# Contiguous destinations for the transposed loads of B and C, and the first x rows in one transfer

## The chip, the cores and the metric

The kernel runs on one core of a Trainium2 chip. The metric is the device time of one execution in microseconds, as a median over runs. Before the change it is 252.53 us, the median of three runs (252.28 to 253.31).

## The reference

A sequence of 2048 tokens with 1024 channels goes through two branches that are mixed by a gate per token, `g = sigmoid(sum(x * gate_w))`; the result is `g * a + (1 - g) * b`.

Branch a is a diagonal state-space layer with complex state of 1024: `Bu = x @ B_bar`, then `h = Lam_bar * h + Bu[t]` over the 2048 tokens, then `y = 2 * Re(h @ C^T) + x * Dskip`. `Lam_bar = exp(dt * Lambda)` and the factor in `B_bar` come from three vectors of length 1024 (`log_dt`, `Lambda_re`, `Lambda_im`).

Branch b picks the 8 tokens with the largest `x @ w_r`, puts only these through a gated expert (`(silu(x w_gate) * (x w_up)) w_down`, hidden size 3584), scales them and adds them to their rows of x.

## The kernel before

The sequence is cut into 8 chunks of 256 tokens, the 1024 channels and the 1024 states into 8 tiles of 128 each. Stage 1 (`s1`, its matmuls are line 253, tile `vps`) multiplies the transposed B, planes re and im, with the transposed x of a chunk; one call `s1(k, cp)` does two state tiles of both planes, 32 matmuls, and ScalarE evicts the PSUM tile to V (line 258). VectorE rotates V by tables (lines 277 to 279), runs the recurrence as a real scan (line 288) and rotates back to H (lines 311 to 315). Stage 2 (`s2`, line 716, tile `zps`) multiplies H with the transposed C, 512 output columns at a time; `s2_last` (line 730) does the last 128 tokens in pieces of 512, 256 and 256 columns. The expert's matmuls (lines 635 and 647), the token selection (lines 501 to 554, tile `fl` among them, read on VectorE at line 533 by `ci`) and the gate columns (`zc`, line 468) are placed between these stages.

The order of the work on TensorE, VectorE, ScalarE and SyncE is written out by hand; each engine runs its list in that order. The main loop over chunks places the pieces by position in a list of pending functions; the first chunks (prologue) are spelled out line by line.

The start matters for the change. SyncE issues, one after the other: the first 256 rows of x as they are (`x0r`, line 77, two transfers), the first two state tiles of B re and B im as transposing transfers (line 89), x of chunks 1 and 2 as transposing transfers (`xT1`, `xT2`, line 85), then the rest of B in pieces of 256 rows and C in pieces of 512 rows (line 98). ScalarE's queue loads the three small vectors into `vrow`. Chunk 0 of x is transposed on TensorE: eight transposes per 128 rows (line 144, tile `xq`), copied to `xT[0]` by ScalarE for the first 128 rows and by VectorE for the second (line 145). Between the two groups stand three small transposes of `vrow` (line 149) and their copy to `vec` on VectorE (line 150). From `vec` follow `dt_b` on ScalarE (line 164), `ang` on VectorE (line 167) and the angle tables (lines 191 to 211). Warm-up matmuls (line 137, tile `wps`) stand ahead of the x transposes (12) and ahead of the first `s1` (7). The prologue's first stage-1 calls are chunk 0, chunk 1 and chunk 2 for the first two state tiles; PSUM has two buffers for `vps`.

BT and CT are one SBUF tile per plane. BT's free dimensions are (channel tile, state); a load of two state tiles writes 256 columns in each of the eight channel tiles, with a step of 1024 elements. CT's are (state tile, output column); a load writes 512 columns in each of eight. The xT tiles are written whole by one transfer each.

The tail of branch b adds the expert rows to the output by one indirect accumulating transfer on GpSimd's queue and reads the last 256 rows back (`ul`, line 703, 128 partitions of two rows).

Of the kernel before, what the change touches and what calls it, by code (L numbers as in the profile page):

```python
# [11 lines left out]
BF16 = mybir.dt.bfloat16  # L12
# [4 lines left out]
P = 128  # L17
LC = 256
# [6 lines left out]
def kernel(  # L25
# [19 lines left out]
    nc = tc.nc  # L45
    _, L, D = A_x.shape
    NP_ = A_B_re.shape[0]
    Fdim = B_w_gate.shape[1]
    NCT = NP_ // P
    KD = D // P  # L50
    NK = L // LC
    NTT = L // P
    BPC = LC // P
    NDH = D // 512
# [4 lines left out]
    x2d = A_x[0]  # L59
    out2d = out[0]  # L60
    Bsrc = (A_B_re, A_B_im)
    Csrc = (A_C_re, A_C_im)

    ctx.enter_context(tc.manual_schedule(engines={mybir.EngineType.PE, mybir.EngineType.DVE, mybir.EngineType.Activation, mybir.EngineType.SP}))
    const = ctx.enter_context(tc.tile_pool(name="const", bufs=1))
# [3 lines left out]
    ps_m = ctx.enter_context(tc.tile_pool(name="ps_m", bufs=2, space=PSUM))  # L69

    xT = [const.tile([P, KD, LC], BF16, name=f"xT{k}", tag=f"xT{k}") for k in range(5)]
    BT = [const.tile([P, KD, NP_], BF16, name=f"BT{pl}") for pl in range(2)]
    CT = [const.tile([P, NCT, D], BF16, name=f"CT{pl}") for pl in range(2)]

    x0r = const.tile([P, BPC, D], BF16, name="x0r", tag="xT5")
    for tl in range(BPC):
        nc.sync.dma_start(x0r[:, tl, :], x2d[tl * P:(tl + 1) * P, :])
    vrow = small.tile([NCT, 5, P], BF16, name="vrow", tag="va")
    for i, v in enumerate((A_log_dt, A_Lambda_re, A_Lambda_im)):
        nc.scalar.dma_start(vrow[:, i, :], v.rearrange("(c p) -> c p", p=P))  # L80
# [5 lines left out]

    def load_B(c0, c1):
        for pl in range(2):
            nc.sync.dma_start_transpose(BT[pl][:, :, c0 * P:c1 * P], Bsrc[pl][c0 * P:c1 * P, :])  # L89

    load_B(0, 2)
    load_xT(1)
# [2 lines left out]
        load_B(c0, c0 + 2)  # L95
    for d0_ in range(0, D, 512):
        for pl in range(2):
            nc.sync.dma_start_transpose(CT[pl][:, :, d0_:d0_ + 512], Csrc[pl][d0_:d0_ + 512, :])

    big_free = [(f"big{i}", "") for i in range(5)]  # L100
    big_tag = {}
# [18 lines left out]
    ident = const.tile([P, P], BF16, name="ident")  # L120
# [20 lines left out]
    for tl in range(BPC):  # L141
        xq = ps_s2.tile([P, KD, P], BF16, name="xq", tag="zps")
        for dc in range(KD):
            nc.tensor.transpose(xq[:, dc, :], x0r[:, tl, dc * P:(dc + 1) * P], ident[:])
        (nc.scalar.copy if tl == 0 else nc.vector.tensor_copy)(out=xT[0][:, :, tl * P:(tl + 1) * P], in_=xq[:])
        if tl == 0:
            va_ps = ps_m.tile([P, 3, NCT], BF16, name="va_ps", tag="m")
            for i in range(3):
                nc.tensor.transpose(va_ps[:, i, :], vrow[:, i, :], ident[:NCT, :NCT])
            nc.vector.tensor_copy(vec[:, 0:3, :], va_ps[:])  # L150
    ldt, lre, lim = vec[:, 0, :], vec[:, 1, :], vec[:, 2, :]


# [93 lines left out]
    def s1u(k, cp, c, pl):  # L247
        if (k, cp) not in vp:
            vp[k, cp] = ps_s1.tile([P, 2, 2, LC], F32, name="vps", tag="vps")
        vps = vp[k, cp]  # L250
        ct = 2 * cp + c
        for dc in range(KD):
            nc.tensor.matmul(vps[:, pl, c, :], lhsT=BT[pl][:, dc, ct * P:(ct + 1) * P], rhs=xT[k][:, dc, :], start=(dc == 0), stop=(dc == KD - 1))  # L253

    def s1e(k, cp):
        if k not in V:
# [451 lines left out]
    def s2(b, dh):  # L708
        k, tl = divmod(b, BPC)
        if dh == 0:  # L710
            ots[b] = opool.tile([P, D], BF16, name="ot", tag="ot")
        dsl = slice(dh * 512, (dh + 1) * 512)
        zps = ps_s2.tile([P, 512], F32, name="zps", tag="zps")
        for ct in range(NCT):
            for pl in range(2):
                nc.tensor.matmul(zps[:], lhsT=H[k][:, pl, ct, tl * P:(tl + 1) * P], rhs=CT[pl][:, ct, dsl], start=(ct == 0 and pl == 0), stop=(ct == NCT - 1 and pl == 1))  # L716
        if dh == 1 and tl == 1:
            big_done("H", k)
        nc.scalar.activation(out=ots[b][:, dsl], in_=zps[:], func=ACT.Copy, scale=gcol[:, b:b + 1])  # L719

    def s2_last(b):
        k, tl = divmod(b, BPC)
        ots[b] = opool.tile([P, D], BF16, name="ot", tag="ot")
        cols = ((0, 512), (512, 256), (768, 256))
        zp = [(ps_s2, ps_s1, ps_s1)[i].tile([P, w], F32, name="zl", tag=("zps", "vps", "vps")[i]) for i, (_, w) in enumerate(cols)]
        for c0 in (0, NCT // 2):
            for i, (d_, w) in enumerate(cols):
                for ct in range(c0, c0 + NCT // 2):
                    for pl in range(2):
                        nc.tensor.matmul(zp[i][:], lhsT=H[k][:, pl, ct, tl * P:(tl + 1) * P], rhs=CT[pl][:, ct, d_:d_ + w], start=(ct == 0 and pl == 0), stop=(ct == NCT - 1 and pl == 1))  # L730
                if c0 and i == 0:
                    nc.scalar.activation(out=ots[b][:, 0:512], in_=zp[0][:], func=ACT.Copy, scale=gcol[:, b:b + 1])
                    fin_half(b, 0)
                elif c0:
                    nc.vector.scalar_tensor_tensor(out=ots[b][:, d_:d_ + w], in0=zp[i][:], scalar=gcol[:, b:b + 1], in1=xts[b][:, d_:d_ + w], op0=ALU.mult, op1=ALU.add)
                    nc.sync.dma_start(out2d[b * P:(b + 1) * P, d_:d_ + w], ots[b][:, d_:d_ + w])
# [147 lines left out]
```

## Time and profile before

| | |
|---|---|
| median of three runs | 252.53 us (252.28 to 253.31) |
| the profiled execution's own time | 252.53 us |
| its span, first to last instruction | 250.8 us |
| TensorE busy | 244.3 us (97%) |
| VectorE busy | 232.9 us (93%) |
| ScalarE busy | 101.6 us (41%) |
| GpSimd busy | 41.3 us (16%) |
| granted TensorE clock | 0.999 |
| chain that ended last | PE 49%, DVE 41%, SP queue 3%, DMA 3%, issue 2% |

PE is TensorE's matmuls, DVE VectorE, ACT ScalarE, POOL GpSimd, SP SyncE; a q behind a name is that engine's queue of instructions or transfers. The chain of waits is followed back from the last instruction: at each step to what released it, or to the instruction before it on its engine. In the timeline the bracket at the end of a line is the idle time of the engine just before it and what ended it. In the windows the columns are busy time and instruction count of PE, weight loads, DVE, ACT and POOL, then the granted clock, the mean busy share of the 16 DMA engines and GB/s. In a tile view the three figures of an instruction are the least, median and greatest duration in ns.

### The profile page before, as it was taken

How to read it: one execution, taken by the hardware profiler on the slowest of the kernel's cores; microseconds unless marked ns; L12 is line 12 of the kernel's file. 1: busy time of each engine (PE TensorE's matmuls, PEld its weight loads, DVE VectorE, ACT ScalarE, POOL GpSimd, SP SyncE). 2: the span in 40 equal slices, each digit the busy share in tenths (PEclk: the TensorE clock that was granted, in tenths of full speed). 3: DMA queues.
4: the chain of work that ended last, by engine and by line, in shares of the span. 5: the costliest groups of instructions: out<-in, count | busy, mean ns of one | idle time of the engine just before them, and what ended most of it. 6: DMA issues, size and time to landing. Idle time of an engine off the chain costs nothing.

```text
span 250.8 us, 4677 instructions
## 1 busy us (share of the span) xinstructions
PE 244.3 (97%) x1986; PEld 164.2 (65%) x1986; DVE 232.9 (93%) x230; ACT 101.6 (41%) x143; POOL 41.3 (16%) x58
## 2 busy tenths in 40 slices
PE   8799999999999999999999999999999999999994
PEld 5688889884678447874487644876448864454453
DVE  1899999999999599999999999999999999999992
ACT  3679981535212322535121372131732335264411
POOL 4020000000000067201400240013101400141520
PEclk9999999999999999999999999999999999999999
DMA  7999999999900202819795587869999829966072
GB/s 182 228 158 238 179 258 211 251 260 261 312 0 3 73 0 89 167 31 348 156 358 190 203 232 236 277 216 338 262 288 293 183 46 277 302 169 178 3 167 84
DMA packets 63492, 48.31 MB, mean 193 GB/s; under 512 B 49504, under 2 KB 51168, under 8 KB 63472
## 3 DMA queue, kind: packets, MB, share of 16 engines
q1 hardware_dynamic: 59056, 37.23, 56.6%
q0 software_dynamic: 4224, 10.53, 17.5%
q8 instruction: 15, 0.25, 0.4%
q10 hardware_dynamic: 192, 0.27, 0.3%
q14 instruction: 5, 0.04, 0.1%
HBM read 27.55 MB, written 8.40 MB: 143 GB/s over the span
## 4 chain that ended last, share of the span: by engine, by line
PE 49%; DVE 41%; SPq 3%; DMA 3%; issue 2%; ACT 0%; DVEq 0%
PE vps L253 22%; PE zps L716 21%; DVE U L288 14%; DVE U L277 4%; DVE U L279 4%; DVE V L278 4%; DVE U L313 4%; DVE H L315 4%; DVE H L311 4%; DVE xt L691 3%; PE zl L730 3%; DMA xT<-in_A_x_dram 3%; SPq L89 2%; PE y L647 1%; PE zc L468 1%
## 5 line engine op out<-in xcount | busy, mean ns | idle before, releaser
L253 PE MATMUL vps<-xT,BT 128*128 128x256 bf16 x1024 | 114.2, 273 | 1.6 <-DMA BT<-in_A_B_re_dram 0.8
L253 PEld LDWEIGHTS <-BT 128*128 128x128 bf16 x1024 | 99.4, 98 | 15.6 <-issue 1.8
L716 PE MATMUL zps<-CT,H 128*128 128x512 bf16 x480 | 105.8, 379 | 0.0
L716 PEld LDWEIGHTS <-H 128*128 128x128 bf16 x480 | 46.3, 98 | 55.7 <-issue 1.9
L288 DVE TENSOR_TENSOR_SCAN U<-d,U 128x2048 bf16<-128x2048 f32 (+1 forms) x20 | 61.7, 3128 | 0.4
L258 ACT CAST V<-vps 128x1024 bf16<-128x1024 f32 x32 | 32.3, 1009 | 60.9 <-PE vps L253 60.9
L719 ACT ACTIVATE ot<-zps,gcol 128x512 bf16<-128x512 f32 x30 | 20.6, 688 | 67.8 <-PE zps L716 65.0
L693 POOL DMA_DIRECT2D out_dram<-xt x14 | 7.8, 561 | 93.1 <-DVE xt L691 92.6
L687 ACT ACTIVATE e<-Dbc,omgcol,gcol 128x1024 f32<-128x1024 bf16 x16 | 18.9, 1233 | 0.0
L691 DVE TENSOR_TENSOR xt<-xt,e 128x1024 bf16<-128x1024 bf16 x16 | 18.8, 1218 | 0.0
L278 DVE TENSOR_TENSOR V<-V,nTi 128x4096 bf16<-128x4096 bf16 (+1 forms) x10 | 16.5, 1652 | 0.5
L277 DVE TENSOR_TENSOR U<-V,T2tab 128x4096 bf16<-128x4096 bf16 (+1 forms) x10 | 16.5, 1645 | 0.5
L279 DVE TENSOR_TENSOR U<-U,V 128x4096 bf16<-128x4096 bf16 (+1 forms) x10 | 16.5, 1652 | 0.3
L554 POOL DMA_INDIRECT xsel<-in_A_x_dram,idx_c x1 | 6.4, 6387 | 61.3 <-ACT ot L719 61.3
L313 DVE TENSOR_TENSOR U<-U,S2tab 128x4096 bf16<-128x4096 bf16 (+1 forms) x8 | 16.2, 2025 | 0.3
L315 DVE TENSOR_TENSOR H<-H,U 128x4096 bf16<-128x4096 bf16 (+1 forms) x8 | 16.2, 2025 | 0.3
L311 DVE TENSOR_TENSOR H<-U,Ctab 128x4096 bf16<-128x4096 bf16 (+1 forms) x8 | 16.1, 2018 | 0.0
L740 POOL DMA_DIRECT2D out_dram<-ot x14 | 14.3, 1048 | 2.0 <-DMA out_dram<-yc,idx_c 2.0
L682 POOL DMA_DIRECT2D xt<-in_A_x_dram x12 | 8.2, 684 | 13.6 <-DMA out_dram<-xt 13.6
L346 DVE TENSOR_TENSOR_SCAN U<-D,U 128x1024 bf16<-128x1024 f32 x4 | 8.9, 2278 | 0.0
L635 PE MATMUL pgu<-wgu,xsel 128*32 128x448 bf16 x128 | 7.4, 355 | 0.0
L730 PE MATMUL zl<-CT,H 128*128 128x256 bf16 (+1 forms) x48 | 7.1, 308 | 0.0
(145 smaller groups left out, 127.9 us busy)
## 6 DMA issues: line engine op xcount, KB each, us to landing
wgu<-in_B_w_gate_dram SPq DMA_DIRECT2D x16, 448.0 KB, 6.4
wgu<-in_B_w_up_dram SPq DMA_DIRECT2D x16, 448.0 KB, 5.7
wd<-in_B_w_down_dram SPq DMA_DIRECT2D x12, 512.0 KB, 6.7
out_dram<-xt POOLq DMA_DIRECT2D x14, 256.0 KB, 2.8
out_dram<-ot POOLq DMA_DIRECT2D x14, 256.0 KB, 5.9
xt<-in_A_x_dram POOLq DMA_DIRECT2D x12, 256.0 KB, 5.1
xt<-in_A_x_dram SPq DMA_DIRECT2D x4, 256.0 KB, 4.1
wd<-in_B_w_down_dram SPq DMA_DIRECT2D x4, 256.0 KB, 7.8
```

Source lines behind the costliest of these rows:

```text
L253: nc.tensor.matmul(vps[:, pl, c, :], lhsT=BT[pl][:, dc, ct * P:(ct + 1) * P], rhs=xT[k][:, dc, :], start=(dc == 0), stop=(dc == KD - 1))
L258: nc.scalar.copy(out=V[k][:, :, 2 * cp:2 * cp + 2, :], in_=vp.pop((k, cp))[:])
L277: nc.vector.tensor_tensor(out=u, in0=v, in1=T2tab[:, :, c0:c1, :], op=ALU.mult)
L278: nc.vector.tensor_tensor(out=v, in0=v, in1=bc(nTi, c0, c1), op=ALU.mult)
L279: nc.vector.tensor_tensor(out=u, in0=u, in1=V[k][:, ::-1, c0:c1, :], op=ALU.add)
L288: nc.vector.tensor_tensor_scan(out=fl, data0=d0[:, c0:c1, :].rearrange("p c t -> p (c t)"), data1=fl, initial=0.0, op0=ALU.mult, op1=ALU.add)
L311: nc.vector.tensor_tensor(out=h, in0=g, in1=bc(Ctab, c0, c1), op=ALU.mult)
L313: nc.vector.tensor_tensor(out=g, in0=g, in1=S2tab[:, :, c0:c1, :], op=ALU.mult)
L315: nc.vector.tensor_tensor(out=h, in0=h, in1=G[k][:, ::-1, c0:c1, :], op=ALU.add)
L691: nc.vector.tensor_tensor(out=xt[:], in0=xt[:], in1=es.pop(b)[:], op=ALU.mult)
L716: nc.tensor.matmul(zps[:], lhsT=H[k][:, pl, ct, tl * P:(tl + 1) * P], rhs=CT[pl][:, ct, dsl], start=(ct == 0 and pl == 0), stop=(ct == NCT ...
L719: nc.scalar.activation(out=ots[b][:, dsl], in_=zps[:], func=ACT.Copy, scale=gcol[:, b:b + 1])
```

## The change

Four edits, all of them in loads and layouts:

- `x0r` is loaded by one transfer of 128 partitions by two rows in place of two transfers of 128 rows.
- The three small transposes of `vrow` and the copy to `vec` come after both groups of x transposes, in place of between them.
- BT's tile is laid out as (pair of state tiles, channel tile, 256 columns), so that each transposing load of B writes one contiguous stretch of each partition; the matmuls of line 253 index it accordingly.
- CT's tile is laid out as (half of the output columns, state tile, 512 columns), with the same effect for the loads of C and the matmuls of stage 2.

The counts of instructions on TensorE, VectorE, ScalarE and GpSimd stay the same; SyncE issues one transfer less. On VectorE the copy of `vec` changes places with the second copy to `xT[0]`.

```diff
-    BT = [const.tile([P, KD, NP_], BF16, name=f"BT{pl}") for pl in range(2)]
-    CT = [const.tile([P, NCT, D], BF16, name=f"CT{pl}") for pl in range(2)]
+    BT = [const.tile([P, NCT // 2, KD, 2 * P], BF16, name=f"BT{pl}") for pl in range(2)]
+    CT = [const.tile([P, NDH, NCT, 512], BF16, name=f"CT{pl}") for pl in range(2)]
 
     x0r = const.tile([P, BPC, D], BF16, name="x0r", tag="xT5")
-    for tl in range(BPC):
-        nc.sync.dma_start(x0r[:, tl, :], x2d[tl * P:(tl + 1) * P, :])
+    nc.sync.dma_start(x0r[:], x2d[0:LC, :].rearrange("(t p) d -> p t d", p=P))
...
-            nc.sync.dma_start_transpose(BT[pl][:, :, c0 * P:c1 * P], Bsrc[pl][c0 * P:c1 * P, :])
+            nc.sync.dma_start_transpose(BT[pl][:, c0 // 2], Bsrc[pl][c0 * P:c1 * P, :])
...
-            nc.sync.dma_start_transpose(CT[pl][:, :, d0_:d0_ + 512], Csrc[pl][d0_:d0_ + 512, :])
+            nc.sync.dma_start_transpose(CT[pl][:, d0_ // 512], Csrc[pl][d0_:d0_ + 512, :])
...
         (nc.scalar.copy if tl == 0 else nc.vector.tensor_copy)(out=xT[0][:, :, tl * P:(tl + 1) * P], in_=xq[:])
-        if tl == 0:
-            va_ps = ps_m.tile([P, 3, NCT], BF16, name="va_ps", tag="m")
-            for i in range(3):
-                nc.tensor.transpose(va_ps[:, i, :], vrow[:, i, :], ident[:NCT, :NCT])
-            nc.vector.tensor_copy(vec[:, 0:3, :], va_ps[:])
+    va_ps = ps_m.tile([P, 3, NCT], BF16, name="va_ps", tag="m")
+    for i in range(3):
+        nc.tensor.transpose(va_ps[:, i, :], vrow[:, i, :], ident[:NCT, :NCT])
+    nc.vector.tensor_copy(vec[:, 0:3, :], va_ps[:])
...
-            nc.tensor.matmul(vps[:, pl, c, :], lhsT=BT[pl][:, dc, ct * P:(ct + 1) * P], rhs=xT[k][:, dc, :], start=(dc == 0), stop=(dc == KD - 1))
+            nc.tensor.matmul(vps[:, pl, c, :], lhsT=BT[pl][:, cp, dc, c * P:(c + 1) * P], rhs=xT[k][:, dc, :], start=(dc == 0), stop=(dc == KD - 1))
...
-                nc.tensor.matmul(zps[:], lhsT=H[k][:, pl, ct, tl * P:(tl + 1) * P], rhs=CT[pl][:, ct, dsl], start=(ct == 0 and pl == 0), stop=(ct == NCT - 1 and pl == 1))
+                nc.tensor.matmul(zps[:], lhsT=H[k][:, pl, ct, tl * P:(tl + 1) * P], rhs=CT[pl][:, dh, ct, :], start=(ct == 0 and pl == 0), stop=(ct == NCT - 1 and pl == 1))
...
-                        nc.tensor.matmul(zp[i][:], lhsT=H[k][:, pl, ct, tl * P:(tl + 1) * P], rhs=CT[pl][:, ct, d_:d_ + w], start=(ct == 0 and pl == 0), stop=(ct == NCT - 1 and pl == 1))
+                        nc.tensor.matmul(zp[i][:], lhsT=H[k][:, pl, ct, tl * P:(tl + 1) * P], rhs=CT[pl][:, d_ // 512, ct, d_ % 512:d_ % 512 + w], start=(ct == 0 and pl == 0), stop=(ct == NCT - 1 and pl == 1))
```

## The prediction

> **What bounds the kernel now.** I read the page's busy shares, then the chain that ended last in order of time, then the timeline of the first 16 us (the only place where the change moves an instruction), and last the tile views of the transposed loads and the windows by stage.
>
> Busy shares: TensorE is the engine with the least room, VectorE next.
>
> ```profile
> PE 244.3 (97%) x1986; PEld 164.2 (65%) x1986; DVE 232.9 (93%) x230; ACT 101.6 (41%) x143; POOL 41.3 (16%) x58
> ```
>
> The chain, in order of time (start, us, what):
>
> ```profile
> 0.74 0.40 SPq L77
> 1.14 0.06 issue
> 1.20 0.42 SPq L77
> 1.62 0.05 issue
> 1.67 2.65 SPq L89
> 4.32 0.05 issue
> 4.37 2.06 SPq L89
> 6.44 0.04 issue
> 6.48 2.11 SPq L85
> 8.58 0.04 issue
> 8.63 6.91 DMA xT<-in_A_x_dram
> 15.54 0.05 issue
> 15.59 24.63 PE vps L253 x224
> ...
> 86.12 0.25 ACT fl L526
> 86.37 0.02 issue
> 86.40 0.28 DVE ci L533
> ```
>
> The reader is to see that the chain enters TensorE at 15.59, when xT2 lands, and that from there TensorE never stops: between 15.6 and 84 us it is busy 68.40 of 68.40 us. At 86.40 the chain passes to VectorE, released by TensorE's work through ScalarE, and returns to TensorE at 194.9. So the time of the whole kernel hangs on when TensorE begins its unbroken run. A later start there is passed on one to one; so is an earlier one.
>
> VectorE has one pause in its stream between 14 and 194 us, and it is the spare room of everything that the change delays:
>
> ```profile
> 86.40 0.28 DVE L533 TENSOR_TENSOR ci<-fl,jrow 8x128 f32<-8x128 f32 x1 [2.45 <-ACT fl L526]
> ```
>
> **The change, part by part.** The sum is made against the profiled execution: span 250.8, its time 252.53, which is also the median of the three runs; 1.73 us lie outside the span.
>
> (a) *One x load in place of two.* SyncE loses one issue, 0.42 + 0.05 = 0.47 us, so every transpose behind it (B, xT1, xT2, then the rest) can be issued up to 0.47 earlier. The chain puts this on the path. But the DMA engines are nearly full then: their share is 0.84 and 0.96 in the windows 2 to 3 and 3 to 4 us (289 and 304 GB/s), and 1.0 to 1.3 in every window from 4 to 13, so the first B transpose stands behind the x rows and each transpose behind the last. The x rows are the same bytes. The gain on xT2's landing is therefore between 0 (the engines are the limit) and 0.47 (the issue is); I take 0.15, near the first, because the full windows are the nearest rows. A loss needs a later landing, below.
>
> When does the merged load land? Before, the halves landed 2.8 us after the issue at 0.74 (3.57) and 3.3 after that at 1.20 (4.5). The ul load has the same shape (128 partitions of 2 rows, 512 KB) and landed after 3.3 us, which gives 4.05; adding 256 KB at 300 GB/s (0.87) to the first landing gives 4.45. I take L = 4.3. The first eight transposes, which started at 3.57, start then; the second eight, which started at 5.02, do not wait for a load of their own any more.
>
> (b) *The transposes of the small vectors behind both x groups.* TensorE before: eight x transposes 3.60 to 4.65, three small ones to 5.08, eight more 5.02 to 5.64, seven warm-up matmuls 5.47 to 6.40. After: sixteen from 4.3 (about 1.05 + 0.62) to 6.0, three small ones (0.5) to 6.5, seven warm-ups (0.93) to 7.4. The first matmuls of L253 started at 7.18, when the first B transpose landed; now they start at about 7.4. Their first half then ends near 9.2, where the second plane's B landed at 9.12, and the group ends near 11.1, before xT1's landing, which was 11.5 and held TensorE up for 0.47. So 0.2 us of delay is eaten by that wait and costs nothing. Without that cover it would cost 0.2.
>
> (c) *VectorE's and ScalarE's start.* VectorE copied vec at 5.12, then the x half at 5.67 to 6.36; ang could start only at 6.28. After, the x half goes first (6.0 to 6.7), vec follows (to about 6.9), dt_b on ScalarE comes 0.29 later and takes 0.21 (to 7.4), ang starts at about 7.45. The tables, and VectorE's whole stream behind them, start about 1.2 us late. Who waits for that? ScalarE: the Sin pair and then the eviction of the first PSUM tile, 12.18 to 13.17, which becomes 13.4 to 14.4; TensorE needs that buffer at 15.3, so 0.9 us remain. ScalarE is caught up at 15.16, where it waited 1.42 for TensorE. VectorE carries the 1.2 on; H of chunk 0 ended at 51.9 and was read at 55.1, H of chunk 1 ended at 75.3 and was read at 81.7 (3.2 and 6.4 to spare), and the 2.45 pause shrinks to about 1.1. Cost: nothing, as long as the delay stays under 2.45.
>
> (d) *Contiguous destinations for B and C.* TensorE reads the same 128-column weights and 512-column operands, contiguous in either layout; its instructions keep their shapes. What is left is the transfer. The kernel has the control in itself: xT tiles are written whole, thus already contiguous, B in pieces of 256 columns with a step of 1024.
>
> ```profile
> L89 SPq DMA_TRANSPOSE BT<-in_A_B_im_dram x4: 1998/2041/2277, 4.4 to 24.1; - x4
> ...
> DMA to landing us min/median/max: 4.7/5.5/6.7
> ```
>
> ```profile
> L85 SPq DMA_TRANSPOSE xT<-in_A_x_dram x7: 1579/2524/2729, 6.5 to 58.8; - x7
> ...
> DMA to landing us min/median/max: 4.6/5.0/5.4
> ```
>
> Same bytes, and the strided ones hold the queue no longer than the contiguous ones (medians 2.04 for one plane of B, 2.55 for the other, 2.52 for xT). Landing is 5.5 against 5.0, partly because two B loads fell into the gap below. I cost this part at nothing; the bounds are 0 and, from the landings, 0.5 per B transpose, two of which stand ahead of xT2: −1.0, which TensorE cannot use in full (below). C is first read at 55 us, long after; nothing there.
>
> The Trainium skill, "DMA: Bandwidth & Descriptors", section "Latency and other measured facts", says that a DMA transpose runs at 261 GB/s with a non-contiguous middle dimension and at about 350 to 400 contiguous. By it the two B transposes would each take some 0.6 us less, and the sum would be the 251.8 of the first rival below; by the rows it is nothing. The same skill's "Trainium Kernel Development and Optimization", section "Best Practices", asks to overlap transfers with compute, which speaks against the merged load: the first eight transposes no longer run under the second half's transfer. By that rule alone the 0.7 us from 3.57 to L would be lost; the waits of (b) cover it.
>
> **Sum.** xT2 lands 0.15 earlier, TensorE's run starts 0.15 earlier, everything behind shifts with it: 252.53 − 0.15 = 252.4. Within 0.5% (1.26 us, about what a measurement of this kernel can tell from no change) on either side by a wide margin.
>
> There is also a floor. TensorE must do two groups of 32 matmuls (3.53 and 3.65 us) and two small transposes (0.2) before xT2's group. With the first group at 7.25 at the earliest (L of 4.05 and the 3.2 us of transposes, vectors and warm-up behind it) the run cannot start before 14.65: at most 0.94 of gain, 0.37%, however fast the transfers get.
>
> **The rivals.**
>
> *Faster transposes.* The contiguous destination, or the earlier issue, really shortens the loads. For it: xT1 and xT2 held TensorE for 0.47 and 0.29, and B for 0.78 and about 0.2. Against it: the two tile views. Price: TensorE from about 7.4 without a wait, 7.4 + 3.53 + 3.65 + 0.2 = 14.8 in place of 15.59, so about −0.75: 251.8. Still within 0.5%. Chance 0.10.
>
> *The merged x load lands late* (the other side). Everything at the start stands behind it: with landing L, TensorE's first group starts at L + 3.1 and must end its two groups by 15.5, so the point is L = 5.0, 0.7 after my value; from there each us costs one, and from L = 5.5 VectorE's 2.45 is gone too. The 512 KB loads of wd took a median of 6.7 us to land under heavy traffic, which bounds it: L = 7.4, 2.4 us later, 254.9. For it: one semaphore now covers twice the bytes, with vector loads of three queues beside it. Against it: the ul row's 3.3 us. It counts as slower (over 1.26) from L = 6.3. Chance 0.07.
>
> *The gap in the transfers falls elsewhere.* In the windows 13 to 14 and 14 to 15 the transfers drop to 68 and 15 GB/s, just as xT2 was finishing; the packet records show a 16 KB packet of the instruction queue (2.0 us) there.
>
> ```profile
> 13.00:14.00 1.00, 1.00 (x11) 0.90 (x10) 0.93 (x10) 0.78 (x3) 0.00 (x0) 1.00 2.27 68
> 14.00:15.00 1.00, 1.00 (x11) 0.79 (x9) 1.00 (x6) 0.00 (x0) 0.00 (x0) 1.00 0.31 15
> ```
>
> If xT2 escapes it, TensorE gains only the 0.29 that it waited: 252.2. If the gap falls ahead of xT1, that lands 2.2 later, at 13.7; 3.65 + 0.2 behind it is 17.6, 2.0 later: 254.5. The packet comes with TensorE's progress, which is still held by xT1's landing, so the order should stay. Chance 0.05 for the bad case.
>
> *Nothing moves at all* (the issue saved is hidden whole): 252.5. It lies inside the forecast.
>
> **How the numbers follow.** Forecast with its variants (252.0 to 252.8): 0.78; faster transposes 0.10 (251.8); late load 0.07 (253.5 to 254.9); displaced gap 0.05 (254.5). Faster by over 0.5% needs more than the floor allows, so only an unseen cause gives it: 0.05, taken out of the first two. Slower by over 0.5%: the two bad cases, some of the late load staying below the bound: 0.10. Same: 0.85. The three runs before spread over 252.28 to 253.31, so the range is 251.6 to 253.4, which leaves out the two bad cases and the unseen gain.
>
> **What would show it.** After: one issue at L77, B's first issue near 1.2; the x transposes starting at 4.0 to 4.5 in one run of sixteen; ang 0.9 to 1.3 later than 6.28; TensorE's unbroken run starting at 15.1 to 15.7; the pause before ci at 0.9 to 1.6 in place of 2.45; B transposes holding the queue 2.0 to 2.6 us as before. It is wrong if B's transposes take 1.5, if the x load lands after 5, or if the pause before ci is gone.

## The result, and the profile after

Measured beside each other, six executions of each, the kernel after takes 253.88 us (253.28 to 254.35) and the kernel before 252.69 (252.28 to 253.31): a ratio of 1.0046, with a 95% interval of 1.0028 to 1.0064. Measured a second time (twelve executions of after, 35 of before) it is 252.84 against 252.59, 1.0025 (1.0006 to 1.0044). The ratios here and below are the recorded ones of the two sets of executions, not quotients of the medians beside them; the medians of the second measurement alone would give 1.0010. By the ratios the change costs 0.25 to 0.46%. That is a small loss, below the 0.5% that the prediction called the same, but both intervals lie above 1, and a gain of 0.15 us was forecast. The first result lies above the range that was given, the second inside it.

The profiled execution of after took 253.81 us with a span of 252.0; before it was 252.53 and 250.8. The span is 1.2 us longer, as the time is (1.28). The counts of instructions have not moved. The busy shares of the page, engine by engine:

```profile
PE 245.4 (97%) x1986; PEld 164.9 (65%) x1986; DVE 233.1 (93%) x230; ACT 101.6 (40%) x143; POOL 41.1 (16%) x58
```

TensorE is busy 1.1 us longer with the same 1986 instructions. That says that something ran slower, not only later. The chain that ended last, of the kernel after, in order of time (start, us, what):

```profile
1.69 5.06 DMA vrow<-in_A_Lambda_im_dram
6.75 0.05 issue
6.80 0.17 PE va_ps L147
6.98 1.40 PE wps L136 x7
8.38 8.12 PE vps L250 x64
16.50 0.13 PE vb_ps L418 x2
16.63 24.56 PE vps L250 x224
```

Before, the chain came through SyncE's queue and the landing of xT2. Now SyncE's transfers are gone from it: from 6.80 on it is TensorE's own work, without a wait. The unbroken run starts about 1 us later (16.63 against 15.59). TensorE's timeline of the same kernel between 3 and 9 us shows the two waits ahead of that (the bracket is the idle time and what ended it):

```profile
4.76 1.07 PE L143 MATMUL xq<-ident,x0r 128*128 128x128 bf16 x16 [0.96 <-DMA x0r<-in_A_x_dram]
5.76 0.20 PE L147 MATMUL va_ps<-ident,vrow 8*128 8x8 bf16 x2
6.80 0.17 PE L147 MATMUL va_ps<-ident,vrow 8*128 8x8 bf16 x1 [0.84 <-DMA vrow<-in_A_Lambda_im_dram]
6.91 1.47 PE L136 MATMUL wps<-wt 128*128 128x256 bf16 x7
8.17 1.06 PE L250 MATMUL vps<-xT,BT 128*128 128x256 bf16 x4
```

The merged x load landed 4.0 us after its issue, and TensorE waited 0.96 for it. Then it waited 0.84 for the third small vector, which before had landed in time. Sixteen x transposes took 1.07, so the clock was full there; the seven warm-up matmuls took 1.47, against 0.93 before. The windows of 1 us of the same kernel tell why (busy time and instruction count of PE, weight loads, DVE, ACT and POOL, then the granted clock, the DMA share and GB/s):

```profile
6.00:7.00 1.00, 0.20 (x2) 0.19 (x3) 0.56 (x1) 0.43 (x1) 0.00 (x0) 1.00 1.04 185
7.00:8.00 1.00, 1.00 (x7) 0.73 (x7) 0.68 (x4) 0.44 (x3) 0.00 (x0) 0.58 1.14 226
8.00:9.00 1.00, 1.00 (x6) 0.72 (x5) 1.00 (x4) 1.00 (x1) 0.44 (x1) 0.50 1.19 253
9.00:10.00 1.00, 1.00 (x7) 0.72 (x5) 0.93 (x3) 0.26 (x1) 0.00 (x0) 0.50 1.23 278
10.00:11.00 1.00, 1.00 (x9) 0.77 (x8) 1.00 (x1) 0.00 (x0) 0.00 (x0) 0.72 1.02 230
11.00:12.00 1.00, 1.00 (x12) 0.90 (x10) 0.93 (x4) 0.95 (x1) 0.00 (x0) 1.00 1.17 267
```

The granted clock of TensorE falls to half from 7.16 to 10.57: by its own records it was full from 3.74, half for 3.41 us, and full from then on. PE is "1.00 busy" in these windows with 6 to 7 matmuls where 12 fit at full clock. A busy share does not show that an engine runs at half rate; the number in brackets and the clock column do.

What the half clock costs can be worked out. At full clock the two groups of 32 matmuls and what stands between them and the run take 7.23 us (7.41 to 14.64 in a kernel below, the base with two loads, whose clock was full there and whose two groups met no wait). Before they took 8.41 (7.18 to 15.59), so 1.18 of it was waiting for B, xT1 and xT2. After they took 8.39 (8.17 to 16.56 in the timeline): no wait is left, and 1.16 of it is the clock. The first group started 0.99 later, the waits gone (−1.18) would have paid for that, and the clock (+1.16) took it back: 0.97. (2.40 us of the two groups lie at half clock, which by itself costs half of that, 1.20.) The last 0.23 of the span's 1.2 is a wait for the expert's `wd` at the end (a group of 56 matmuls took 1.94 at 222.39, and 1.71 before).

VectorE's pause, which the forecast had as the spare room, in the timeline of the kernel after:

```profile
87.37 0.28 DVE L530 TENSOR_TENSOR ci<-fl,jrow 8x128 f32<-8x128 f32 x1 [2.11 <-ACT fl L523]
```

It is 2.11 in place of 2.45, though VectorE's stream started about 1.2 late: TensorE, whose work releases this step through ScalarE, is about 1 us late too. B's transposes, in the tile view (least, median and greatest ns that a transfer held the queue):

```profile
L88 SPq DMA_TRANSPOSE BT<-in_A_B_re_dram x4: 2010/2364/3381, 1.3 to 20.5; - x4
L88 SPq DMA_TRANSPOSE BT<-in_A_B_im_dram x4: 1858/2060/3207, 4.7 to 23.0; - x4
...
DMA to landing us min/median/max: 4.5/4.8/6.6
```

One plane went from 2546 (the 2.55 of the prediction) to 2364, the other from 2041 to 2060. The first B transpose, issued at 1.26 in place of 1.67, landed 6.6 us later, at 7.87; before it had landed at 7.13. So the earlier issue brought no earlier landing here, but a later one. Whether the layout does anything is for the experiments.

The gap in the transfers, which stood at 13 to 15 us before, has moved. In the windows of the kernel after, the low rates come two windows later:

```profile
15.00:16.00 1.00, 1.00 (x11) 0.89 (x10) 0.97 (x7) 0.10 (x1) 0.00 (x0) 1.00 1.80 92
16.00:17.00 1.00, 1.00 (x11) 0.71 (x9) 0.97 (x3) 0.46 (x1) 0.31 (x1) 1.00 0.51 80
```

So xT2 was ahead of the gap: by the landing records it was in at 13.45, where before it came at 15.54 and was what the run waited for.

The second measurement's profile (252.91, span 251.1) has the same cause in another phase. The wait for x is 1.05, the vectors are in time, and the clock is at half from the beginning until 9.08, so that the x transposes take 1.89 and the warm-ups 1.67:

```profile
4.86 1.89 PE L143 MATMUL xq<-ident,x0r 128*128 128x128 bf16 x16 [1.05 <-DMA x0r<-in_A_x_dram]
...
6.85 1.67 PE L136 MATMUL wps<-wt 128*128 128x256 bf16 x7
8.31 7.53 PE L250 MATMUL vps<-xT,BT 128*128 128x256 bf16 x64
...
15.91 24.63 PE L250 MATMUL vps<-xT,BT 128*128 128x256 bf16 x224
```

Here only the first 0.77 us of the two groups lie at half clock; the groups take 0.37 more than the 7.23 of full clock, and the run starts 0.32 later than before. The expectation of this run, which came with a later group of experiments:

> The changed kernel once more, for its scatter and a second profile. Theory S as it stands after the first four (the single x load makes TensorE start late and lose the full clock for one window of 3.4 us; the span is TensorE's unbroken start plus 235.2): 253.3 to 254.0, and the profile shows the clock at half until about 10, with the run starting at 16.2 to 16.8; where the clock happens to hold, 15.4 to 15.8 and a span near 250.8. Rival W (the weights for the expert's second matmul come late, as in the first profile, 0.2 us): the same start as before and the loss near 223.

It measured 252.84, below the 253.3 that was expected at the least; the half clock until about 10 was nearly met (9.08), the start of 16.2 to 16.8 was not (15.91). In both profiles the changes of the clock lie on a grid of 3.41 us (in the first at 3.74, 7.16 and 10.57), but the grid of the second is shifted against it: counted back from 9.08 it has edges at 5.67 and 2.26. The two profiles' start times differ with that phase; that the two medians differ for the same reason isn't shown.

### The profile page after: what moved, and what is told of

The parts are those of the page before. It is cut to its first block, busy times and chain, and to the rows that moved or that the text cites. A ratio compares the mean times of both kernels' runs of the same rounds, so it can differ in the third digit from the quotient of the medians.

```text
span 252.0 us, 4675 instructions
## 1 busy us (share of the span) xinstructions
PE 245.4 (97%) x1986; PEld 164.9 (65%) x1986; DVE 233.1 (93%) x230; ACT 101.6 (40%) x143; POOL 41.1 (16%) x58
## 4 chain that ended last, share of the span: by engine, by line
PE 48%; DVE 41%; DMA 7%; issue 2%; ACT 0%; ACTq 0%; DVEq 0%
PE vps L250 25%; PE zps L713 17%; DVE U L285 14%; DMA wd<-in_B_w_down_dram 5%; DVE V L275 4%; DVE U L276 4%; DVE U L274 4%; DVE H L312 4%; DVE U L310 4%; DVE H L308 4%; DVE xt L688 3%; PE zl L727 3%; DMA vrow<-in_A_Lambda_im_dram 2%; PE zc L465 1%; PE y L644 1%
## 5 line engine op out<-in xcount | busy, mean ns | idle before, releaser
L310 DVE TENSOR_TENSOR U<-U,S2tab 128x4096 bf16<-128x4096 bf16 (+1 forms) x8 | 16.2, 2025 | 0.3
L312 DVE TENSOR_TENSOR H<-H,U 128x4096 bf16<-128x4096 bf16 (+1 forms) x8 | 16.2, 2025 | 0.3
```

The source lines that it names most:

```text
L310: nc.vector.tensor_tensor(out=g, in0=g, in1=S2tab[:, :, c0:c1, :], op=ALU.mult)
L312: nc.vector.tensor_tensor(out=h, in0=h, in1=G[k][:, ::-1, c0:c1, :], op=ALU.add)
```

## The experiments

Theories after the result: the merged x load makes TensorE idle at the start, and the clock falls; or the new layout makes the first B transposes late; or the moved small transposes delay VectorE. First, each part of the change alone, on the kernel before.

**The layout alone.**

```diff
-    BT = [const.tile([P, KD, NP_], BF16, name=f"BT{pl}") for pl in range(2)]
-    CT = [const.tile([P, NCT, D], BF16, name=f"CT{pl}") for pl in range(2)]
+    BT = [const.tile([P, NCT // 2, KD, 2 * P], BF16, name=f"BT{pl}") for pl in range(2)]
+    CT = [const.tile([P, NDH, NCT, 512], BF16, name=f"CT{pl}") for pl in range(2)]
...
-            nc.sync.dma_start_transpose(BT[pl][:, :, c0 * P:c1 * P], Bsrc[pl][c0 * P:c1 * P, :])
+            nc.sync.dma_start_transpose(BT[pl][:, c0 // 2], Bsrc[pl][c0 * P:c1 * P, :])
```

> The contiguous layouts of B and C alone; two x loads and the vectors between the x groups as before. Theory S (the slower time comes from the start alone: x and the vector loads land later, TensorE stands idle twice and its clock is granted at half for one more window of 3.4 us): 252.7, the kernel before within 0.3. Rival L (the layout itself costs, in the transposes or in the matmuls that read it): 253.9, B's transposes longer than 2.0 to 2.6 us of queue.

Measured: 252.62 us, ratio 1.0005 (0.9985 to 1.0025). No effect that can be measured. Its tile view of B:

```profile
L89 SPq DMA_TRANSPOSE BT<-in_A_B_re_dram x4: 2447/2624/3403, 1.7 to 20.6; - x4
L89 SPq DMA_TRANSPOSE BT<-in_A_B_im_dram x4: 1798/1995/2530, 4.5 to 23.1; - x4
...
DMA to landing us min/median/max: 4.6/5.5/6.8
```

Medians of 2624 and 1995 stand beside 2546 and 2041 with the strided destination, and landing is 5.5 in both.

**The merged load alone.**

```diff
-    for tl in range(BPC):
-        nc.sync.dma_start(x0r[:, tl, :], x2d[tl * P:(tl + 1) * P, :])
+    nc.sync.dma_start(x0r[:], x2d[0:LC, :].rearrange("(t p) d -> p t d", p=P))
```

> The single x load alone; layouts as before, the vectors still between the two x groups. Theory S: B's transposes are issued 0.4 us earlier and pass the third vector load, which lands near 6.7 in place of 4.9; TensorE waits for x until 4.7 and for the vector between its two x groups; 253.5 to 254.5. Rival V (what costs is that VectorE's tables start later because the vectors stand behind both groups): 252.7.

Measured: 253.46 us, 1.0038 (1.0011 to 1.0065): a loss as large as that of the whole change, within the intervals, comes from this one line. It is a little under the 253.5 to 254.5 that was expected, and the vector's wait was shorter (0.22). TensorE's timeline of this kernel:

```profile
4.25 1.03 PE L143 MATMUL xq<-ident,x0r 128*128 128x128 bf16 x8 [0.45 <-DMA x0r<-in_A_x_dram]
...
5.66 0.18 PE L148 MATMUL va_ps<-ident,vrow 8*128 8x8 bf16 x1 [0.22 <-DMA vrow<-in_A_Lambda_im_dram]
5.77 1.03 PE L143 MATMUL xq<-ident,x0r 128*128 128x128 bf16 x8
6.60 1.70 PE L136 MATMUL wps<-wt 128*128 128x256 bf16 x7
8.09 8.21 PE L252 MATMUL vps<-xT,BT 128*128 128x256 bf16 x64
```

The load landed at 4.2, inside the bounds of the prediction, and TensorE idled only 0.45 and 0.22 us. Yet everything in these lines runs at half rate (eight transposes 1.03 where 0.62 is full rate), up to 10.24, and the run starts at 16.36.

**The move alone.**

```diff
-        if tl == 0:
-            va_ps = ps_m.tile([P, 3, NCT], BF16, name="va_ps", tag="m")
-            for i in range(3):
-                nc.tensor.transpose(va_ps[:, i, :], vrow[:, i, :], ident[:NCT, :NCT])
-            nc.vector.tensor_copy(vec[:, 0:3, :], va_ps[:])
+    va_ps = ps_m.tile([P, 3, NCT], BF16, name="va_ps", tag="m")
+    for i in range(3):
+        nc.tensor.transpose(va_ps[:, i, :], vrow[:, i, :], ident[:NCT, :NCT])
+    nc.vector.tensor_copy(vec[:, 0:3, :], va_ps[:])
```

> The vectors behind both x groups alone; two x loads, layouts as before. Theory S: B's transposes are issued at 1.67 as before, the vectors land before 5, TensorE has no wait for them; 252.7 within 0.3. Rival V: ang about 0.7 to 1.2 later, 253.5 to 253.9.

Measured: 252.38 us, 1.0002 (0.9982 to 1.0022). No effect that can be measured. The pause before `ci` was 0.90:

```profile
86.06 0.28 DVE L532 TENSOR_TENSOR ci<-fl,jrow 8x128 f32<-8x128 f32 x1 [0.90 <-ACT fl L525]
```

This doesn't test step (c) at its full size: `ang` came only 0.37 later (6.65 in place of 6.28), not 1.2, and the pause is 0.89 with the layout alone, where VectorE's order is as before. That a delay of 1.2 costs nothing is to be seen in the profile of the whole change, where TensorE's run waits for nothing from VectorE that it did not wait for before.

**The changed kernel with TensorE kept busy.** Five more warm-up matmuls ahead of the x transposes, and the seven later ones ahead of the small transposes. The late load stays, the idle time ahead of the x transposes does not.

```diff
-    warm(12)
+    warm(17)
...
+    warm(7)
     va_ps = ps_m.tile([P, 3, NCT], BF16, name="va_ps", tag="m")
...
     tab_neg(0)
-    warm(7)
```

> The changed kernel with TensorE's waits filled: 17 warm-up matmuls ahead of the x transposes in place of 12, and the later 7 ahead of the vectors' transposes in place of behind them. The loads land as in the changed kernel. Theory S: TensorE has no long idle time, the clock stays full from its first window, the first group of L250 starts near 7.2 and the unbroken run near 14.6; 251.5 to 252.5, faster than the kernel before. Rival V or L: 253.9, as the changed kernel, since neither the layout nor VectorE's start is touched.

The time missed the expectation: 253.01 us, 1.0032 (1.0005 to 1.0059). The start went part of the way that was expected: the clock was full from 4.30 on, and the run began at 15.19, earlier than before's 15.59 but later than the 14.6 expected, because TensorE waited 0.95 for the first B transpose and began its first group at 7.71, not 7.2. In this profile the gain was lost at 52 us:

```profile
52.31 3.67 PE L251 MATMUL vps<-xT,BT 128*128 128x256 bf16 x32 [0.82 <-DMA xT<-in_A_x_dram]
```

TensorE came to `xT3` before it had landed. One profile doesn't tell how often this wait falls there; issuing `xT3` and `xT4` earlier in this kernel was not tried.

**The kernel before, made to idle without touching a load.** Its seven warm-up matmuls after the x transposes are left out; they compute nothing that is used.

```diff
     tab_neg(0)
-    warm(7)
```

> The kernel before without its 7 warm-up matmuls ahead of the first group of L253; nothing in the loads changes. Theory S (the clock is what turns an idle TensorE at the start into time): idle for about 1.5 us in one piece before the first group, the clock at half until about 8 to 10.5 in part of the executions, 253.0 to 253.9. Rival D (the loads' landing alone sets TensorE's start): 252.7, as before, since no load moves.

Measured: 252.75 us, 1.0016 (0.9991 to 1.0041), not told apart from no change in the median. That is below the 253.0 to 253.9 of the theory and at the 252.7 of its rival. The profiled execution (253.3) shows the mechanism all the same. In its timeline TensorE idles 0.61 for a vector and then 1.28 for B:

```profile
7.34 8.83 PE L253 MATMUL vps<-xT,BT 128*128 128x256 bf16 x64 [1.28 <-DMA BT<-in_A_B_re_dram]
...
16.23 24.63 PE L253 MATMUL vps<-xT,BT 128*128 128x256 bf16 x224
```

and its windows have the half clock, from 7.81 to 11.22, again 3.41 us:

```profile
7.00:8.00 1.00, 0.66 (x6) 0.55 (x7) 1.00 (x4) 0.98 (x2) 0.00 (x0) 0.90 1.26 278
8.00:9.00 1.00, 1.00 (x6) 0.70 (x5) 0.93 (x3) 0.48 (x1) 0.00 (x0) 0.50 1.47 198
9.00:10.00 1.00, 1.00 (x7) 0.70 (x5) 1.00 (x1) 0.00 (x0) 0.00 (x0) 0.50 0.93 183
10.00:11.00 1.00, 1.00 (x7) 0.67 (x6) 0.93 (x4) 0.86 (x1) 0.00 (x0) 0.50 1.05 237
```

The first group started at 7.34, only 0.16 later than before; the run started 0.64 later. The executions of this kernel fall in two groups by mean granted clock: four at 0.992 to 0.993 take 253.30 to 254.98, eight at 1.0 take 251.79 to 253.55. So idle time at this place, with the loads of the kernel before, is followed by the half clock in some executions. The mean clock is no test by itself: the second profile of after has a mean of 1.000 although its transposes run at half rate until 9.08, because its clock records begin only there.

**The changed kernel without the wait for the vector.** In after's profile both waits had a share. This run takes the second away: `Lambda_im` goes on SyncE's queue, behind x and ahead of B.

```diff
-        nc.scalar.dma_start(vrow[:, i, :], v.rearrange("(c p) -> c p", p=P))
+        (nc.sync if i == 2 else nc.scalar).dma_start(vrow[:, i, :], v.rearrange("(c p) -> c p", p=P))
```

> The changed kernel with the third vector's load (Lambda_im) issued on SyncE's queue between the x load and B's first transposes, in place of third on ScalarE's queue. Theory S: it lands near 4.5 in place of 5.6 to 6.8, TensorE's wait for it (0.84) goes, the wait for x (0.4 to 1.0) stays; the first group of L250 starts near 7.3, the clock is lost less often; 252.7 to 253.3. Rival X (x's later landing alone is the loss): 253.5 to 253.9, as the changed kernel.

Measured: 253.07 us, 1.0028 (1.0013 to 1.0042). The vector's wait is gone and the loss stays:

```profile
4.75 1.89 PE L143 MATMUL xq<-ident,x0r 128*128 128x128 bf16 x16 [0.95 <-DMA x0r<-in_A_x_dram]
```

with half clock until 9.61 and the run from 16.11. The first group came at 8.20, not near 7.3 as expected. In this profile the wait for x was enough.

**Towards a better kernel.** Two x loads, the contiguous layout, `xT3` and `xT4` ahead of the second half of C, nine late warm-ups in place of seven.

```diff
     for d0_ in range(0, D, 512):
+        if d0_:
+            load_xT(3)
+            load_xT(4)
...
-    warm(7)
+    warm(9)
...
-    load_xT(3)
-    load_xT(4)
     for b in range(4):
```

> Two x loads and the vectors between the x groups as before, B and C contiguous, 9 warm-up matmuls ahead of the first group in place of 7, and xT3 and xT4 transposed ahead of the second half of C in place of behind it. Theory S with the span as TensorE's start plus 235.2: the start at 14.8 to 15.3 in most executions and no wait at 52; 251.8 to 252.4, faster than the kernel before by 0.1 to 0.3%. If the start is not what counts: 252.7.

Measured: 252.71 us, 1.0006 (0.9991 to 1.0021). That misses the expectation and is the value named for the case that the start is not what counts. Its profile, of one of the three fastest executions, is early (run from 15.00, 251.93 in all), its median is not: no gain that can be measured.

**The cost of the merged load where the transposed loads hold nothing up.** The four kernels that follow are a base of their own: the transposing loads of B, C and of x from chunk 1 on are plain loads of the same bytes, so those transposes are left out. They differ among each other only in what is named below. First, with two x loads:

```diff
-        nc.sync.dma_start_transpose(xT[k][:], x2d[k * LC:(k + 1) * LC, :])
+        nc.sync.dma_start(xT[k][:].rearrange("p a b -> p (a b)").rearrange("p (t d) -> p t d", d=D), x2d[k * LC:(k + 1) * LC, :].rearrange("(t p) d -> p t d", p=P))
...
-            nc.sync.dma_start_transpose(BT[pl][:, c0 // 2], Bsrc[pl][c0 * P:c1 * P, :])
+            nc.sync.dma_start(BT[pl][:, c0 // 2].rearrange("p a b -> p (a b)").rearrange("p (t d) -> p t d", d=D), Bsrc[pl][c0 * P:c1 * P, :].rearrange("(t p) d -> p t d", p=P))
```

> The base of a pair without transposing transfers: two x loads and the vectors between the x groups as before, contiguous B and C, but B, C and x of chunks 1 to 7 are loaded with the same bytes untransposed, so the result is not the layer's; the instructions of all engines are the same. Expected of both theories: TensorE's first x transpose near 3.6, its run's start at 14.8 or earlier, 251.0 to 252.5.

Measured: 250.90 us (250.24 to 253.9), ratio 0.9939 (0.9907 to 0.9970). Against it the merged load:

```diff
-    for tl in range(BPC):
-        nc.sync.dma_start(x0r[:, tl, :], x2d[tl * P:(tl + 1) * P, :])
+    nc.sync.dma_start(x0r[:], x2d[0:LC, :].rearrange("(t p) d -> p t d", p=P))
```

> As the base of the pair (transposes of B, C and x chunks 1 to 7 left out), with the single x load. Theory S: the first x transpose at 4.2 to 4.9, the clock at half up to 7 to 10 in many executions, 0.3 to 1.2 us over the base. Rival T (the single load costs only because transposing transfers stand behind it): the base within 0.2.

Measured: 252.05 us (251.48 to 254.07), 1.15 more than the base; the ratio, 0.9972 (0.9941 to 1.0004), has an interval that overlaps with the base's, but the fastest of these twelve executions is slower than eight of the base's twelve. The two profiles are of executions slower than their medians (251.55 and 253.33). The two timelines of TensorE, first the base with two loads:

```profile
3.60 0.69 PE L144 MATMUL xq<-ident,x0r 128*128 128x128 bf16 x8
...
7.41 7.16 PE L252 MATMUL vps<-xT,BT 128*128 128x256 bf16 x64 [1.65 <-DMA BT<-in_A_B_re_dram]
```

then with one:

```profile
4.15 1.04 PE L143 MATMUL xq<-ident,x0r 128*128 128x128 bf16 x8 [0.34 <-DMA x0r<-in_A_x_dram]
...
8.13 8.15 PE L251 MATMUL vps<-xT,BT 128*128 128x256 bf16 x64
```

The first group starts 0.72 later and its 64 matmuls take 8.15 in place of 7.16, 0.99 more, at half clock until 10.17: together the run starts 1.70 later (16.34 against 14.64). With two loads TensorE still waited 1.65 for B, and the 0.55 by which x came later is less than that wait. What goes beyond it is a wait of 0.37 for the vector, the transposes and warm-ups at half rate, and the 0.99. So the loss does not need the transposing loads behind x.

**Lateness without a merged load.** Two loads, but the transposes begin with the second 128 rows, which land later.

```diff
-    for tl in range(BPC):
+    for tl in (1, 0):
...
-        (nc.scalar.copy if tl == 0 else nc.vector.tensor_copy)(out=xT[0][:, :, tl * P:(tl + 1) * P], in_=xq[:])
-        if tl == 0:
+        (nc.scalar.copy if tl == 1 else nc.vector.tensor_copy)(out=xT[0][:, :, tl * P:(tl + 1) * P], in_=xq[:])
+        if tl == 1:
```

> As the base of the pair (transposes of B, C and x chunks 1 to 7 left out), two x loads, with the x groups in the other order, rows 128 to 255 first: TensorE waits for the second load, and no load moves. Theory S (the wait for x and the clock lost through it is the loss): 0.3 to 1.0 over the base, like the single load. Rival Q (the earlier issue of the loads behind x is the loss): the base within 0.2.

Measured: 252.05 us (250.96 to 252.81), also 1.15 over the base: no load is merged or moved, and the median loses as much. But the profile is of the fastest execution (250.96). There TensorE idled 0.31 and 0.22, the clock was full from 4.96, and the run began at 14.03. So it doesn't show what the others lost; that it was the clock is an inference from the series, not shown. The same order on the kernel before was not tried.

**The merged load with the wait filled.** The merged-load kernel of this base with 17 warm-ups in place of 12.

```diff
-    warm(12)
+    warm(17)
```

> As the single load of the pair (transposes of B, C and x chunks 1 to 7 left out), with 17 warm-up matmuls ahead of the x transposes in place of 12. Theory S: TensorE is busy up to x's landing, the clock is full by 4 to 7.4, and half or more of the loss against the base is gone. Rival M (the single load costs in a way that TensorE's start does not show): as the single load.

Measured: 251.81 us (251.53 to 252.68), ratio 0.9955 (0.9934 to 0.9977): 0.24 of the 1.15 is back, which the scatter of twelve executions does not tell from nothing. Half or more was expected, so this missed, and the times leave the rival M standing. The profile, of one of the three slowest executions (252.62), shows the start whole: the clock is full from 5.47 and the run begins at 14.58, as in the base's profile. What it loses there is later, at loads that TensorE meets before they have landed:

```profile
156.53 0.37 PE L633 MATMUL pgu<-wgu,xsel 128*32 128x448 bf16 x4 [0.56 <-DMA wgu<-in_B_w_gate_dram]
...
180.75 0.37 PE L633 MATMUL pgu<-wgu,xsel 128*32 128x448 bf16 x4 [0.64 <-DMA wgu<-in_B_w_up_dram]
```

**All profiles together.** "Idle" is TensorE's idle time between its first matmul and the first group; "full from" is where the clock records begin, or where the last half-clock stretch ends. Times are from the start of the span.

| kernel | x loads | idle, us | clock full from | run starts | span | ratio to before |
|---|---|---|---|---|---|---|
| before | 2 | 0.2 + 0.78 | 4.51 | 15.59 | 250.8 | |
| after, first | 1 | 0.96 + 0.84 | 3.74, then half 7.16 to 10.57 | 16.56 | 252.0 | 1.0046 |
| after, second | 1 | 1.05 | 9.08 | 15.91 | 251.1 | 1.0025 |
| layout alone | 2 | 0.56 + 0.35 | 3.80 | 14.76 | 250.6 | 1.0005 |
| merge alone | 1 | 0.45 + 0.22 | 10.24 | 16.36 | 251.6 | 1.0038 |
| move alone | 2 | 0 | 6.41 | 15.25 | 250.4 | 1.0002 |
| after, filled | 1 | 0.95, just before the group | 4.30 | 15.19 | 251.4 | 1.0032 |
| before, 7 fewer warm-ups | 2 | 0.61 + 1.28 | 4.39, then half 7.81 to 11.22 | 16.23 | 251.5 | 1.0016 |
| after, vector on SyncE | 1 | 0.95 | 9.61 | 16.11 | 251.3 | 1.0028 |
| towards better | 2 | 0.21 | 6.27 | 15.00 | 250.1 | 1.0006 |
| base, two loads | 2 | 1.65, just before the group | 3.75 | 14.64 | 249.8 | 0.9939 |
| base, one load | 1 | 0.34 + 0.37 | 10.17 | 16.34 | 251.6 | 0.9972 |
| base, second rows first | 2 | 0.31 + 0.22 | 4.96 | 14.03 | 249.2 | 0.9961 |
| base, one load, filled | 1 | 0 | 5.47 | 14.58 | 250.8 | 0.9955 |

All five profiles with one x load and no filling have half clock until 9.1 to 10.6. All with two loads and all the warm-ups, and both filled ones, are full from 6.41 at the latest. And in all fourteen, the span less the start of the run less the later waits of TensorE for loads is between 234.9 and 235.4: what happens before the run, and those waits, is the whole difference between these profiles. The later waits are 0.23 (after, first), 0.83 (layout alone), 0.82 (after, filled), 0.36 (7 fewer warm-ups) and 1.20 (base, one load, filled).

How much of the late start is the clock can be worked out for the six profiles with half clock inside the two groups: half of the time that the groups spend at half clock, against what they take beyond 7.23. It is 1.20 against 1.16 (after, first), 0.39 and 0.37 (after, second), 1.08 and 1.04 (merge alone), 0.71 and 0.68 (vector on SyncE), 1.71 and 1.66 (7 fewer warm-ups), 1.02 and 0.98 (base, one load). The clock accounts for the whole excess.

When it changes can be read from the same records. In every trace the changes of the clock lie a whole number of times 3.413 us apart, and the grid that they make starts at another phase in each. Cut along its own grid, each profile's windows show how busy TensorE was just before a change (eight of them in the table). Ahead of the first record, "half" is told by the durations alone (228 ns for a warm-up in place of 133).

| kernel | window, us | TensorE busy in it, us | clock in it | clock in the next |
|---|---|---|---|---|
| after, second | 2.26 to 5.67 | 2.36 | half | half |
| after, vector on SyncE | 2.78 to 6.20 | 2.47 | half | half |
| merge alone | 3.42 to 6.83 | 2.74 | half | half |
| layout alone | 0.39 to 3.80 | 2.74 | half | full |
| base, second rows first | 1.54 to 4.96 | 3.11 | half | full |
| after, first | 3.74 to 7.16 | 1.62 | full | half |
| before, 7 fewer warm-ups | 4.39 to 7.81 | 1.53 | full | half |
| base, two loads | 3.75 to 7.16 | 2.01 | full | full |

No window at half clock with 2.47 us busy or less was followed by the full clock, every one with 3.11 or more was; between 2.68 and 2.74 both happen. At the start, the full clock was lost after the two windows with least work, 1.53 and 1.62, and kept after 2.01 and more. The order is rough: at the end of the span, where other matmuls run, it was kept after windows with 1.48, 1.65 and 1.75 and lost after 1.37. So what a wait costs goes with where the grid's edges fall: of the wait of 1.65 in the base with two loads, which did not lose the clock, only 1.40 lies in one window, while the 1.80 and 1.89 of idle time of the two that lost it lie in one window each.

## Why the prediction was wrong

The frame held in the profiles: a profile's span does hang on when TensorE's unbroken run begins, one to one, as the table's constant shows. The failing step is (b): its sum has TensorE at full clock from the late x load on, and puts nothing down for the clock.

- **(a), the earlier issue: no gain.** B's first issue came at 1.26 in place of 1.67, near the 1.2 that was expected. But the packet records have its first packet at 3.63, against 3.62 before, and it landed at 7.87 and 7.36 in the two profiles, against 7.13. So the 0.15 was not gained. That xT2 landed about 2 us earlier is due to the gap, below, and nothing waited for it. The landing L = 4.3 was also too small for most profiles: 4.1 to 4.2 in three of the merged-load kernels, but 4.7 to 4.8 in both profiles of after, beyond the upper bound of 4.45.
- **(b), TensorE's start: wrong, and this is what decides.** The first group was put at 7.4 and came at 8.17 and 8.31. Of that, 0.46 and 0.56 is the later landing (transposes from 4.76 and 4.86 in place of 4.3); the rest, 0.31 and 0.35, comes behind it, from the vector's wait in the first profile and from transposes and warm-ups at half rate in the second. The cover was right: with the later start the waits for B, xT1 and xT2 vanished, all 1.18 us of them. With a full clock in the two groups the run would have started at 8.17 + 7.23 = 15.40, or 8.31 + 7.23 = 15.54, by which time xT2 was in (13.45 and 13.55): no later than before's 15.59, and by this sum the late load would have been free. The term that failed is the duration behind it: the two groups and the small transposes were put at 3.53 + 3.65 + 0.2 = 7.38, full rate, and took 8.39 and 7.60, which is 1.16 and 0.37 over the 7.23 measured at full clock. All durations of the step came from rows where the clock was full or became full, and they were carried to a start with a hole in it, where it wasn't. What the clock does was in the rows of before: eight x transposes took 1.05 and then 0.62, and a warm-up 228 ns (2.74 for 12) and then 133 (0.93 for 7). The sum used both without asking why they differ.
- **(c), VectorE's later start: right.** `ang` was put at 7.45 and came at 7.47 and 7.84. The 7.47 is partly luck: the copy of the x half began at 5.87, earlier than put, and a wait of 0.46 for the late vector made up for it. The pause before `ci`, put at about 1.1, was 2.11 and 0.43, and so never used up. The move alone costs nothing that can be measured.
- **(d), the layout: right.** 1.0005 (0.9985 to 1.0025).
- **The rival of the late load: the right line, the wrong mechanism.** It was priced as lateness, from a point of L = 5.0. The loss came at L = 4.1 to 4.8, by way of the clock: in the merge alone L was 4.2 and the run started later than in the second profile of after, where L was 4.8. By its rule, first group at L + 3.1, the merge alone would have begun at 7.3; it began at 8.09. What is paid for is idle time in a window of the clock, more than the lateness itself.
- **The gap in the transfers: wrong, without a cost.** It was to stay at 13 to 15 us, because xT1's landing holds TensorE there. In the profile of after it came at 15 to 17, behind xT2's landing. That is the branch in which xT2 escapes it, worth 0.29 by the prediction; since TensorE was later than xT2, it was worth nothing.

The rule that was not weighed: the Trainium skill, "TensorE: Matmul & The Clock Gate", Part 1, has the clock at half by default and after an idle window, full after a busy one, with free-running windows of 4096 cycles, 3413 ns. The two half-clock stretches here, 3.41 us each, and the grid agree with it. Where the page speaks of an idle window, these traces show that it need not be idle throughout: 1.80 and 1.89 us of idle time in one of 3.41 lost the full clock.

Open: why the two measurements of after differ (1.0046 and 1.0025), since the mean clock of an execution doesn't show a half clock at its start; what the median of the kernel with the second rows first lost; and why none of the three kernels that were to win the start back (both filled ones and the one with two loads and nine warm-ups) is as fast by its median as the start in its profile would have it. The later waits in two of their profiles are one answer, but one profile each doesn't show how often they fall there. So the clock as the cause is shown in the profiles and their sums; by medians only the merged load is.

## What to carry to other kernels

At the start of a kernel, the first thing to protect is that TensorE is not idle: a load that it meets should come in pieces, so that the first piece can be worked on while the second lands, and merging two issues saved nothing here, where the transfer engines were already full. When the same instructions take two different durations in one profile, find out why before using either in a sum; here the pair was the clock. And a start that becomes earlier is only worth what the later loads allow: in their profiles both filled kernels gave it back at waits for later loads, at 52 us in one and at 156 and 181 us in the other.

## What was not expected of the hardware

- The clock changed only at the edges of a grid of 3.413 us, at another phase in each execution, and at the start the change went with how busy TensorE had been in the window just past (the second table above). That isn't a sharp rule of the idle time: 0.67 to 0.72 us in a window kept the clock from rising in merge alone and in base, one load, but not in layout alone. What tells these apart (the small transposes, the place of the idle time) is not shown by any run here.
- A 2 KB load, issued at 1.69 on ScalarE's queue, landed 5.06 us later in the first profile of after, where B's transpose was issued at 1.26; before, with B issued at 1.67, it took about 3.2. In the second profile it was in time. By the landing records it came at 5.6 to 6.8 in the six profiles with a merged x load and this queue, and at 4.1 to 5.3 in the seven with two x loads; issued on SyncE's queue ahead of B it came at 4.2. That the larger transfers on the other queue hold it up is a reading of this; no run separates it from the merged load itself.
- The same merged load of 512 KB took 3.4 (twice), 3.5, 3.9, 4.0 (twice) and 4.1 us to land in seven profiles; the halves of 256 KB took 2.6 to 3.3 in before and in two kernels of the base.
